# Sliding-window attention and gated MLP layers on one core: masked-Q score tiles, joined bursts and a new order

## Chip, cores and metric

The kernel runs on one NeuronCore of a Trainium2 chip. The metric is device time in microseconds (us) of one execution. The engines are TensorE (PE; its weight loads are listed apart as PEld), VectorE (DVE), ScalarE (ACT), GpSimd (POOL) and SyncE (SP, which here only issues DMAs). Each runs its own instructions in order; between engines they wait on semaphores.

## What is computed

Four layers over x of 2048 tokens by 448 features in bf16: attention (layer 0), MLP (1), attention (2), MLP (3), each on a layer norm of x and added to x. Attention has 16 heads of 28; a token sees itself and 7 earlier tokens at steps of 2.

```python
def attn(x, wqkv, wo):                     # S=2048, D=448, H=16, Dh=28
    q, k, v = split_heads(x @ wqkv)
    idx = pos[:, None] - arange(8) * 2     # 8 keys, every second token
    logits = einsum("hsd,hswd->hsw", q, k[:, idx]) * Dh ** -0.5
    logits = where(idx >= 0, logits, -1e9)
    o = einsum("hsw,hswd->hsd", softmax(logits), v[:, idx])
    return merge_heads(o) @ wo

def mlp(x, w_gate, w_up, w_down):          # F=1792
    return ((x @ w_gate) * (x @ w_up)) @ w_down

x = x + attn(layernorm(x), wqkv, wo)
x = x + mlp(layernorm(x), w_gate, w_up, w_down)
x = x + attn(layernorm(x), wqkv, wo)
x = x + mlp(layernorm(x), w_gate, w_up, w_down)
```

## The kernel before

**Layout and tiles.** Tokens are stored with the even ones first and then the odd ones, so that a step of 2 becomes a step of 1 and the window is the 8 last rows of one half. x lies in SBUF for the whole run. The features (448 = 7 x 64) are contracted in slices of 64, so nearly all matmuls use half of PE's rows: two matmuls, one on rows 0 to 63 and one on rows 64 to 127, run at the same time into two PSUM banks. This is the mode that the code calls `MAIN` ("R64", tiles of 64 rows by 128 columns). `twin` and `twin_blocks` build such pairs and `crossed` chains them, so that after the first half of a pair's slices the two row halves swap outputs. Their instructions are recorded at L698 (Q, K and V projections) and L714 (output projection with `wo_g`, down projection with `WD`). The gate and up matmuls (L983, `b_chunk`) run the same way: 14 units of 7 pairs for each chunk of 256 or 512 tokens.

**Attention.** Queries are handled in 17 blocks of 120 (the first 128), two blocks a group, nine groups a layer. For a group `attn_front` computes the scores: for each of 4 head quadruples, 2 blocks, 2 halves of 64 keys and 4 heads, one matmul (L862) with the 28 rows of one head's K as weights (64 keys as columns) and 64 queries (72 for block 0) moving. That is 64 matmuls in tiles of 28 (32) rows by 64 columns, eight running at once, mode "R32", into four banks (one per head of a quadruple). ACT takes the exponential out of PSUM (L869), DVE multiplies by the band mask `MK` (L879). `attn_back` multiplies by V: 64 matmuls (L896) in tiles of 64 rows by 32 columns, mode "C32". V carries columns of ones, so the sum of the weights comes out beside the values. ACT or DVE copies the result to `O_sb` (L910), DVE adds the overlap (L914), and `norm` spreads the sums (L924, DVE), inverts them by Ln and Exp (L925, L926, ACT) and multiplies (L937, DVE) into `oT`, from which `y_blocks` does the output projection.

**Layer norm and transposes.** `ln_chunk` computes statistics (L630, L632 on DVE; L633, L635 on ACT) and writes the normalized block to a slot of `xn_sb` (L651, DVE). Layers 1 to 3 are transposed by DMA (L654, issued on SP). Layer 0's 16 blocks are transposed by PE, four 128x128 matmuls against `ident` for each (L660, mode "F", one bank), and ACT or DVE copies them to `xnTa` (L666).

**Order.** `SEQ` lists the chunks of layers; `Sched` is a planner that runs while the program is built. Every step is an operation with the engines that may do it, its estimated time, what it depends on, and a priority (by chunk `JP`, by kind `PR`). The planner simulates the engines, and at each moment gives a free engine the ready operation with the lowest priority number; a change of PE's mode costs `SWITCH`. PSUM banks (8) are handed out by the planner (`pick_banks`), SBUF slots by rings (`ring`). The order that comes out is fixed: `emit` writes each engine's instructions in this order, with the waits in front of each operation. PE's instructions of one operation are never mixed with another's.

```python
est = op.est[e]
if e == "pe":
    if mode is not None and op.mode != mode:
        est += self.SWITCH
    mode = op.mode
    n = 2 * len(op.ins)
    credit = min(self.CREDIT, credit + (now - clast) / self.FETCH)
    if n > 40:
        est = max(est, (n - credit) * self.FETCH + (self.HICCUP if n > credit + 40 else 0.0))
```

The head of the program loads x and the weights, and runs 48 warm-up matmuls of 256 columns on zeros (L565).

Of the kernel before, what the change touches and what calls it, by code (L numbers as in the profile page):

```python
# [27 lines left out]
MAIN = "R64"  # L28
PE_T = ("00", "01", "02", "03", "04")
HEAD_LN = 5  # L30
HEAD_P = (-53.71, -30.23, -20.33, -12.94, -19.33)
HOLD_A = 1000.0
HOLD_BA = 2000.0
HOLD_BB = 500.0
HOLD_N = 2
S_EST = 270.0
# [8 lines left out]
NXN_ = 6  # L45
NO = 4
NE_ = 2
NR_ = 3
# [3 lines left out]
PR = {'AV': 8.84, 'rstd': -5.66, 'bn': 0.73, 'N': -2.82, 'Gps': -1.08, 'Tps': 16.85, 'H': 18.16, 'S': 10.61, 'VT': 19.61, 'Ex': 16.77, 'G': -2.93, 'xn': -6.19, 'QK': -6.56, 'Ddps': -26.52, 'V': 22.93, 'x': -0.84, 'lnv': -15.5, 'Oc': -6.51, 'Oa': -6.47, 'R': -19.3, 'VVps': 1.22, 'Yps': -25.3, 'PW': 58.69, 'T': -9.57, 'mv': 2.02, 'Rs': -2.57, 'Rl': 21.52, 'QKps': 4.71, 'E': -7.15, 'wqk': -9.31, 'wqp': -11.53}  # L52
JP = {'A20': -3.02, 'B32': 16.28, 'B34': 16.21, 'A22': 20.13, 'B13': 2.73, 'A21': 6.27, 'B12': -2.81, 'A02': -0.21, 'A03': 4.03, 'B30': 4.3, 'B31': 8.23, 'B10': 21.86, 'B11': -14.15, 'A23': 29.86, 'A04': -0.79, 'B33': 153.62, 'A01': -5.33, 'B14': 4.53, 'A00': -24.6}
# [10 lines left out]
WARM = 18  # L64
FILL = 30
SEED = 190
JITTER = 0
ATT_P = 1.96
A_CAP = 4
# [43 lines left out]
class Op:  # L113
    __slots__ = ("engs", "ins", "est", "deps", "mode", "prio", "acquire", "release", "idx", "eng",
                 "dma", "lat", "after", "start", "end", "seen", "selfd", "tmin")
# [14 lines left out]
class Sched:  # L130
# [6 lines left out]
    SWITCH = 92.0  # L137
    FETCH = 4.17
    CREDIT = 36.0
    HICCUP = 210.0  # L140

    def __init__(self):
        self.ops = []
        self.ready = {}
        self.rng = random.Random(SEED)

    def add(self, engs, ins, est, deps=(), prio=0.0, mode=None, acquire=None, release=(), dma=None, lat=0.0, after=None, selfd=(), tmin=None):
        if isinstance(engs, str):
            engs = (engs,)
        if not isinstance(est, dict):  # L150
            est = {e: float(est) for e in engs}
        op = Op(engs=engs, ins=ins, est=est, deps=[d for d in deps if d is not None], mode=mode, prio=prio,
                acquire=acquire, release=release, idx=len(self.ops), dma=dma, lat=lat, after=after, selfd=set(selfd), tmin=tmin)
# [63 lines left out]

    def schedule(self):
        self.holder = [None] * NBK
# [5 lines left out]
        credit, clast = self.CREDIT, 0.0  # L225
# [6 lines left out]
        for op in self.ops:  # L232
# [9 lines left out]
            if not srcs:  # L242
                for e in op.engs:
                    pend[e].append(op)
        left = len(self.ops)
        now = 0.0
        while left:
            moved = False
            b_ready = any(o.acquire is not None and o.acquire.kind == 1 for o in pend["pe"])
            for e in self.ENGS:  # L250
# [4 lines left out]
                for op in pend[e]:  # L255
                    r = self.ready_at(op, e)
                    if r <= now + 1e-6:
                        cands.append((op.prio, op.idx, op))
# [40 lines left out]
                if best is None:  # L299
                    continue  # L300
                op = best
                op.eng = e
                for x in op.engs:
                    pend[x].remove(op)
                if op.acquire is not None:
                    op.acquire.b = self.pick_banks(op.acquire, now)
                    for b in op.acquire.b:
                        self.holder[b] = op.acquire
                        if self.last_rel[b] is not None:
                            op.deps.append(self.last_rel[b])  # L310
                if op.tmin is not None and e == "sp":
                    gate = [o for o in order["pe"] if o.end + self.PE_LAT <= now and isinstance(o.ins[-1][1], tuple) and o.ins[-1][1] in self.ready]
                    op.deps.append(gate[-1].ins[-1][1])
                est = op.est[e]
                if e == "pe":
                    if mode is not None and op.mode != mode:
                        est += self.SWITCH
                    mode = op.mode
                    n = 2 * len(op.ins)
                    credit = min(self.CREDIT, credit + (now - clast) / self.FETCH)  # L320
                    if n > 40:
                        est = max(est, (n - credit) * self.FETCH + (self.HICCUP if n > credit + 40 else 0.0))
                    credit = max(0.0, credit + est / self.FETCH - n)
                    clast = now + est
                op.start, op.end = now, now + est
                free[e] = op.end
                order[e].append(op)
                for bk, i in op.release:
                    b = bk.b[i]
                    assert self.holder[b] is bk  # L330
                    self.holder[b] = None
                    self.free_at[b] = op.end + self.TAIL[op.eng]
                    key = ("rel", op.idx, b)
                    self.ready[key] = (op, len(op.ins) - 1)
                    self.last_rel[b] = key
                left -= 1
                moved = True
                for u in users.get(op.idx, ()):
                    ndep[u.idx] -= 1
                    if ndep[u.idx] == 0:  # L340
                        for x in u.engs:
                            pend[x].append(u)
# [80 lines left out]
def pe_cols(n):  # L423
    return n / 2.4 + 2.6
# [14 lines left out]
def build(nc, A_x, A_wqkv, A_wo, B_w_gate, B_w_up, B_w_down, out):  # L439
# [52 lines left out]
    def one(fn, key=None):  # L492
        return [(fn, key)]
# [641 lines left out]
```

## Time and profile before

| | before |
|---|---|
| runs | 394.56 us median of 3 (391.71, 394.56, 394.9) |
| profiled execution, span from first to last instruction | 391.9 us |
| DVE busy: 0-10, 10-60, 60-110, 110-250, 250-392 us | 6.3, 46.4, 42.4, 92.2, 83.9 us |
| ACT busy: the same stretches | 4.5, 42.1, 31.4, 67.0, 62.4 us |
| gate and up matmuls (L983) | 1960, 180.5 us |
| down projection (L714, `WD`) | 840, 84.0 us |
| Q and K projection (L698, `WQK`) | 504, 53.5 us |
| output projection (L714, `wo_g`) | 256, 29.1 us |
| V projection (L698, `WV`) | 252, 22.2 us |
| scores (L862) and values (L896) | 1088 each, about 12 us each |
| transposes on PE (L660) | 64, 5.0 us |
| granted TensorE clock | 1.00 in all stretches |

The profile is of one execution. A group's busy time is the union of its instructions' times. Matmuls overlap each other, so the length shown for a matmul is much longer than the time until the next one starts; costs on PE are better read from one start to the next. "Idle before" is the time that an engine stood before an instruction, with what ended it; "issue" stands for time in which it waited for nothing that the profile shows. "PE's weight loads" are separate instructions, one before each matmul.

### The profile page before, as it was taken

The page shows a single profiled execution, that of the slowest core. Times are in us where ns is not written, and L with a number is a line of the kernel's source. Part 1 is how long each engine was busy: PE and PEld are TensorE (multiplying, and loading weights), DVE is VectorE, ACT ScalarE, POOL GpSimd, SP SyncE. Part 2 cuts the span into 40 slices and gives each one's busy share as a digit, 9 for nine tenths or more (in the row PEclk, how much of TensorE's full clock was granted, in tenths as well). Part 3 has the DMA queues.
Part 4 walks back from the last instruction along what each step waited for, and adds up shares of the span by engine and source line. Part 5 has one row for each costly group of instructions (what it writes and reads, how often), then busy time and mean ns, then how long its engine had stood idle before and what let it go on. Part 6 is the DMA issues. An engine that isn't in the chain of part 4 may idle for free.

```text
span 391.9 us, 13910 instructions
## 1 busy us (share of the span) xinstructions
PE 384.9 (98%) x6142; PEld 213.8 (55%) x6142; DVE 271.2 (69%) x596; ACT 207.3 (53%) x398; POOL 7.6 (2%) x36
## 2 busy tenths in 40 slices
PE   8999999999999999999999999999999999999997
PEld 6655657545444544554546867444454544444674
DVE  6989899669967765684788645258942689477252
ACT  4888876478523745467651523268315782263230
POOL 6010000000000000000000000000000000000000
DMA  8990161501220401320121141010050102403101
GB/s 275 295 306 19 24 93 28 106 13 30 48 49 15 80 15 35 64 28 15 17 49 21 36 95 29 25 20 11 12 128 7 26 7 47 95 4 16 34 27 47
DMA packets 54703, 22.47 MB, mean 57 GB/s; under 512 B 44836, under 2 KB 54644, under 8 KB 54644
## 3 DMA queue, kind: packets, MB, share of 16 engines
q1 hardware_dynamic: 53284, 19.47, 23.7%
q10 hardware_dynamic: 1360, 2.12, 1.8%
q8 instruction: 48, 0.79, 0.8%
q14 instruction: 11, 0.09, 0.1%
HBM read 8.54 MB, written 2.71 MB: 29 GB/s over the span
## 4 chain that ended last, share of the span: by engine, by line
PE 90%; DVE 4%; DMA 2%; ACT 2%; issue 1%; SPq 0%; DVEq 0%
PE ps L983 41%; PE ps L714 25%; PE ps L698 16%; PE ps L896 3%; PE ps L862 3%; PE ps L1004 1%; DMA xnTb<-xn_sb 1%; DMA x_sb<-in_A_x_dram 1%; PE ps L660 1%; DVE xn_sb L651 1%; DVE st L630 1%; DVE x_sb L954 1%; ACT R_sb L925 1%; ACT R_sb L926 1%; DVE E_sb L879 0%
## 5 line engine op out<-in xcount | busy, mean ns | idle before, releaser
L983 PE MATMUL ps<-xnTb,WGU 64*128 64x512 bf16 (+1 forms) x1960 | 180.5, 333 | 0.9 <-DMA xnTb<-xn_sb 0.9
L983 PEld LDWEIGHTS ps<-xnTb,WGU 64*128 64x128 bf16 x1960 | 93.5, 94 | 73.8 <-ACT g_sb L989 1.5
L989 ACT ACTIVATE g_sb<-ps 128x512 bf16<-128x512 f32 (+1 forms) x140 | 71.4, 511 | 95.0 <-PE ps L983 94.3
L992 DVE TENSOR_TENSOR hT<-g_sb,ps 128x512 bf16<-128x512 bf16 (+1 forms) x140 | 79.3, 574 | 55.1 <-ACT g_sb L989 46.1
L714 PE MATMUL ps<-WD,hT 64*128 64x448 bf16 x840 | 84.0, 349 | 0.1
L714 PEld LDWEIGHTS ps<-WD,hT 64*128 64x128 bf16 x840 | 40.2, 94 | 37.0 <-DVE hT L992 0.8
L698 PE MATMUL ps<-xnTa,WQK 64*128 64x512 bf16 (+1 forms) x504 | 53.5, 353 | 0.3
L954 DVE TENSOR_TENSOR x_sb<-x_sb,ps 128x448 bf16<-128x448 bf16 x62 | 36.2, 614 | 24.9 <-PE ps L714 24.8
L630 DVE BATCH_NORM_STATS2 st<-x_sb 128x6 f32<-128x448 bf16 x64 | 37.5, 615 | 2.7 <-DMA x_sb<-in_A_x_dram 2.7
L869 ACT ACTIVATE E_sb<-ps 128x1024 bf16<-128x1024 f32 (+1 forms) x36 | 33.5, 980 | 9.6 <-PE ps L862 9.3
L750 ACT ACTIVATE qk<-ps 128x1024 bf16<-128x1024 f32 (+1 forms) x30 | 27.1, 921 | 19.3 <-PE ps L698 19.0
L651 DVE TENSOR_SCALAR xn_sb<-x_sb,mv,rstd 128x512 bf16<-128x512 bf16 (+1 forms) x64 | 33.7, 569 | 4.7 <-ACT rstd L635 4.5
L698 PEld LDWEIGHTS ps<-xnTa,WQK 64*128 64x128 bf16 x504 | 23.5, 94 | 24.0 <-ACT xnTa L666 0.8
L879 DVE TENSOR_TENSOR E_sb<-E_sb,MK 128x1024 bf16<-128x1024 bf16 (+2 forms) x40 | 23.9, 613 | 8.8 <-ACT E_sb L869 8.5
L714 PE MATMUL ps<-wo_g,oT 64*128 64x448 bf16 x256 | 29.1, 349 | 0.0
L633 ACT ACTIVATE lnv<-mv,eps_sb 128x2 f32<-128x2 f32 (+1 forms) x33 | 9.5, 293 | 30.4 <-DVE mv L632 30.2
L937 DVE TENSOR_TENSOR oT<-O_sb,R_sb 128x480 bf16<-128x480 f32 (+3 forms) x36 | 22.1, 627 | 3.4 <-ACT R_sb L926 3.1
L925 ACT ACTIVATE R_sb<-R_sb 128x480 f32<-128x480 f32 (+1 forms) x34 | 20.1, 600 | 5.6 <-DVE R_sb L924 5.6
L924 DVE STREAM_SHUFFLE R_sb<-O_sb 128x480 f32<-128x480 f32 (+1 forms) x34 | 22.7, 696 | 0.0
L698 PE MATMUL ps<-WV,xnTa 64*128 64x336 bf16 (+3 forms) x252 | 22.2, 304 | 0.2
L926 ACT ACTIVATE R_sb<-R_sb 128x480 f32<-128x480 f32 (+1 forms) x34 | 20.1, 602 | 0.4
L714 PEld LDWEIGHTS ps<-wo_g,oT 64*128 64x128 bf16 x256 | 12.3, 94 | 11.6 <-DVE oT L937 0.4
(47 smaller groups left out, 170.7 us busy)
## 6 DMA issues: line engine op xcount, KB each, us to landing
out_dram<-x_sb SPq DMA_DIRECT2D x15, 112.0 KB, 1.7
WD<-in_B_w_down_dram SPq DMA_DIRECT2D x2, 784.0 KB, 11.5
WGU<-in_B_w_up_dram SPq DMA_DIRECT2D x2, 784.0 KB, 17.6
WGU<-in_B_w_gate_dram ACTq DMA_DIRECT2D x2, 784.0 KB, 13.3
x_sb<-in_A_x_dram SPq DMA_DIRECT2D x3, 448.0 KB, 6.4
vt<-qk SPq DMA_DIRECT2D x42, 16.0 KB
xnTb<-xn_sb SPq DMA_TRANSPOSE x32, 3.0
x_sb<-in_A_x_dram SPq DMA_DIRECT2D x2, 224.0 KB, 4.2
```

Of the source, the lines that this page charges most:

```text
L630: sc.add("dve", one(lambda E, B=B: E.bn_stats(st6[:, B, :], x_sb[:, B, :]), ("bn", li, B)), 525.0, deps=[("x", li - 1, B)] + ([("xn", li - ...
L651: sc.add("dve", one(lambda E, B=B, dst=dst, src=src: E.tensor_scalar(dst, src, mv[:, B, 0:1], rstd[:, B:B + 1], ALU.subtract, ALU.mult), ( ...
L698: parts[0 if s < 3 else 1][1].append((lambda E, w=w, c=c, lo=lo, st=st, sp_=sp_: E.matmul(u["out"](w), u["lhs"](w, c, lo, lo + 64), u["rhs ...
L714: ins.append((lambda E, w=w, c=c, lo=lo, st=st, sp_=sp_: E.matmul(outs(w), lhs(w, c, lo), rhs(w, c, lo), start=st, stop=sp_), keys[w] if s ...
L750: return E.activation(dst, src, ACT.Copy) if hasattr(E, "activation") else E.tensor_copy(dst, src)
L869: return E.activation(E_sb[:, slot, 2 * hp:2 * hp + 2, 0:w], ps[:, b0:b0 + 2, 0:w], ACT.Exp, scale=SCALE)
L925: sc.add("act", one(lambda E: E.activation(R_sb[:, rs, 0:w], R_sb[:, rs, 0:w], ACT.Ln), ("Rl", li, qb)), act_est(w, False), deps=[("Rs", l ...
L926: sc.add("act", one(lambda E: E.activation(R_sb[:, rs, 0:w], R_sb[:, rs, 0:w], ACT.Exp, scale=-1.0), ("R", li, qb)), act_est(w, False), de ...
L954: sc.add("dve", one(lambda E: E.tensor_tensor(x_sb[:, B, :], x_sb[:, B, :], ps[:, bk[w], 0:D], ALU.add), ("x", li, B)), dve_est(D), deps=[ ...
L983: ins.append((lambda E, u=u, k=k, w=w: E.matmul(u["out"](w), WGU[64 * w:64 * w + 64, k, 128 * u["fc"]:128 * u["fc"] + 128], X[64 * w:64 * ...
L989: sc.add("act", one(lambda E, gs=gs, bk=bk: E.activation(g_sb[:, gs, 0:nt], ps[:, bk[0], 0:nt], ACT.Copy), ("G", li, j, fc)), act_est(nt), ...
L992: sc.add("dve", one(lambda E, gs=gs, bk=bk, fc=fc: E.tensor_tensor(hT[:, fc, hs, 0:nt], g_sb[:, gs, 0:nt], ps[:, bk[1], 0:nt], ALU.mult), ...
```

## The change

- **Scores.** A new DVE operation per group writes `Qz`, two copies of the group's Q, each with the rows of two of the four heads set to zero (`qmask`, a column of ones and zeros per copy; two `tensor_scalar` instructions of 4 x 240 elements). There is one buffer (`NZ` = 1). A score matmul then takes 64 rows of K (two heads) and 32 keys as weights and moves both masked copies, 2 x 64 queries, so that both heads' scores come out side by side. There are still 64 matmuls per group, now in tiles of 64 rows by 32 columns, the same as the values have; `e_at` says where a head's scores lie. Each pair of banks now holds one query block, and the mask product is one instruction per pair for all groups.
- **Bursts.** Scores and values share the mode `BURST`. When the planner picks one of them, it joins up to `JOIN` = 3 that are ready and, if a projection or gate/up operation (the host) is ready too, puts up to `MAXALT` = 3 of its first steps among them. Such a step, a pair of 64x128 matmuls, is issued as 8 matmuls of 64x32 (`pair`, `alt_of`), one to each column strip. All waits of the joined operations stand in front of the first instruction.
- **Planner.** `run_pe` estimates PE's time from a queue of 64 instructions, a time per instruction, a refill time, and blocks of 256 instructions that arrive after `LINE_T`. In place of the rule with `CREDIT`.
- **Transposes of layer 0.** In chunks 1 to 4 (14 of 16 blocks) each 128x128 transpose becomes two of 64 rows, into two banks, in the mode `MAIN`.
- **Slots.** `xn_sb` 6 to 5, `R_sb` 3 to 2. The values' matmuls now wait for their `O_sb` slot (before, the copy did). Dependences on the last of several matmuls become dependences on all of them; gate/up units keep their order (`after`).
- **Order.** New `PR`, `JP`, `HEAD_P`, `HOLD_*`, `ATT_P` (1.96 to 3.0), `A_CAP` (4 to 5), and a new table `XP` that adds its own priority to most single operations. Warm-up: 25 matmuls of 512 columns in place of 48 of 256.

```diff
 MAIN = "R64"
+BURST = "C32"
+JOIN = 3
+MAXALT = 3
+T64 = (1, 2, 3, 4)
-S_EST = 270.0
+S_EST = 448.0
+AV_EST = 288.0
-NXN_ = 6
+NXN_ = 5
-NR_ = 3
+NR_ = 2
+NZ = 1
-WARM = 18
-FILL = 30
+WARM = 9
+FILL = 16
...
+    QUEUE = 64
+    REFILL = 256.0
+    LINE = 256
+    LINE_T = 3900.0
...
+                    if op.mode == BURST:
...
+                        for o in okay:
+                            if o is not op and o.mode == BURST and len(got) < JOIN and fits(o):
+                                take(o)
+                                got.append(o)
+                        short = [(o, n) for o in got for n in range(len(o.ins))]
+                        n, stream = 2 * len(short), sum(o.est[e] for o in got)
+                        host = next((m for m in okay if m not in got and m.mode == MAIN and len(m.alt) and fits(m)), None)
+                        k = 0
+                        if host is not None:
+                            per = host.est[e] / (len(host.ins) / 2)
+                            while k < len(host.alt) and stream + k * per < self.REFILL + (n + 16 * k - self.QUEUE) * self.FETCH:
+                                k += 1
+                        end = self.run_pe(t, n + 16 * k, stream + (k * per if k else 0.0))
...
+def pair(calls):
...
+    def strip(out, lhs, rhs, start, stop, row, c):
+        return lambda E: E.matmul(out()[c:c + 32], lhs()[:, c:c + 32], rhs(), start=start, stop=stop, tile_position=(row, c))
+    ins = [(whole(*a[:5]), a[6]) for a in calls]
+    strips = [strip(*a[:6], c) for a in calls for c in range(0, 128, 32)] if all(a[6] is None for a in calls) else None
+    return ins, strips
...
+                for c in () if wide else range(4):
+                    for h in range(2):
+                        ins.append((lambda E, c=c, h=h, slot=slot, bk=bk: E.transpose(ps[:, bk[h], :].bitcast(bf)[:, 64 * c:64 * c + 64], xn_sb[64 * h:64 * h + 64, slot, 128 * c:128 * (c + 1)],
+                                                                                      ident[64 * h:64 * h + 64, 64 * h:64 * h + 64]), ("Tps", li, B) if (c, h) == (3, 1) else None))
...
+        def fz(E, a):
+            return E.tensor_scalar(Qz[:, zs, a, :, 0:end - tok], qk[:, 1, :, tok:end], qmask[:, a:a + 1], None, ALU.mult)
...
-        for hc, d, c, b in [(hc, d, c, b) for hc in range(4) for d in range(nd) for c in range(2) for b in range(4)]:
+        for hc, d, c, s_, p in [(hc, d, c, s_, p) for hc in range(4) for d in range(nd) for c in range(2) for s_ in range(2) for p in range(2)]:
             ck, nk, cq, nq = qb_info(qbs[d])
...
+            ins.append((lambda E, hc=hc, c=c, s_=s_, p=p, b=b, h=h, ks=ks, qs=qs: E.matmul(
+                ps[64 * c + 32 * s_:64 * c + 32 * s_ + 32, bk[b], 2 * nc * h:2 * nc * (h + 1)], qk[64 * p:64 * p + 64, 0, hc, ks:ks + 32],
+                Qz[64 * p:64 * p + 64, zs, :, hc, qs:qs + nc], start=True, stop=True, tile_position=(64 * p, 64 * c + 32 * s_)), None))
...
-        sc.add("pe", ins, S_EST * nd / 2, deps=deps + [prev], mode="R32", acquire=bk, prio=prio)
+        sc.add("pe", ins, S_EST * nd / 2 * nc / 64, deps=deps + [prev, ("Qz", li, g)], mode=BURST, acquire=bk, prio=prio)
...
-        xslot_users[hs] = [("Gps", li, j, FC - 1), ("Ups", li, j, FC - 1)]
+        xslot_users[hs] = [(k, li, j, fc) for k in ("Gps", "Ups") for fc in range(FC)]
```

## The prediction

> **What bounds the kernel now.** I read the page's busy table, the chain of waits and the instruction queue first. Columns: engine, busy us, share of the span, instructions.
>
> ```profile
> span 391.9 us, 13910 instructions
> PE 384.9 (98%) x6142; PEld 213.8 (55%) x6142; DVE 271.2 (69%) x596; ACT 207.3 (53%) x398; POOL 7.6 (2%) x36
> ...
> q8 instruction: 48, 0.79, 0.8%
> ...
> PE 90%; DVE 4%; DMA 2%; ACT 2%; issue 1%; SPq 0%; DVEq 0%
> ```
>
> TensorE (PE) carries the chain. It issues 6142 matmuls and as many weight loads, 12284 in all; the instruction queue moved 48 packets of 0.79 MB / 48 = 16 KB, so one packet goes with 12284 / 48 = 256 PE instructions: a block.
>
> Next, PE's timeline around attention. Columns: start, length, engine and line, names, tile shape, count, in brackets the idle time.
>
> ```profile
> 86.78 0.54 PE L896 MATMUL ps<-E_sb,v_sb 64*32 64x64 bf16 x47
> 88.09 0.26 PE L896 MATMUL ps<-E_sb,v_sb 64*32 64x64 bf16 x17 [0.78 <-issue]
> 88.28 1.69 PE L983 MATMUL ps<-xnTb,WGU 64*128 64x512 bf16 x14
> ...
> 179.83 3.19 PE L983 MATMUL ps<-xnTb,WGU 64*128 64x512 bf16 x28
> 182.94 0.71 PE L862 MATMUL ps<-qk 28*64 28x64 bf16 x64
> 183.58 4.71 PE L983 MATMUL ps<-xnTb,WGU 64*128 64x512 bf16 x42
> 188.22 0.71 PE L862 MATMUL ps<-qk 28*64 28x64 bf16 x64
> 188.86 3.20 PE L983 MATMUL ps<-xnTb,WGU 64*128 64x512 bf16 x28
> 191.98 1.36 PE L896 MATMUL ps<-E_sb,v_sb 64*32 64x64 bf16 x128
> 193.27 6.22 PE L983 MATMUL ps<-xnTb,WGU 64*128 64x512 bf16 x56
> ```
>
> The wide matmuls cannot get faster: 183.58 to 188.22 holds 21 pairs, 4.64 us less one drain of 0.1, which is 0.216 us a pair and so 0.42 ns a column. The attention bursts can. From 179.83, 14 pairs end at 182.85, the scores start at 182.94 and the next wide matmul at 183.58: one score burst costs 0.09 + 0.64 = 0.73 us. The double value burst costs 0.10 + 1.29, so 0.70 each. At 88.09 a value burst stood 0.78 us for "issue", with no semaphore behind it.
>
> Where a burst's time goes, by counting its matmuls in windows that grow (window, length, PE busy and count, clock, DMA):
>
> ```profile
> 182.90:183.10 0.20, 0.16 (x32) 1.00 0.18 21
> 182.90:183.20 0.30, 0.26 (x35) 1.00 0.22 24
> 182.90:183.30 0.40, 0.36 (x47) 1.00 0.21 23
> 182.90:183.40 0.50, 0.46 (x59) 1.00 0.22 25
> ```
>
> 32 matmuls (64 instructions) start within 0.16 us, then almost none for 0.1 us, then 12 per 0.1 us: 8.3 ns for a matmul and its load. The second half is paced by instruction supply, not by the array.
>
> Last, the other engines by stage, and the DVE groups nearest to the new operation (busy us, mean ns, idle before).
>
> ```profile
> 10.00:60.00 50.00, 48.89 (x1092) 28.94 (x1086) 46.42 (x119) 42.07 (x82) 1.64 (x6) 1.00 0.60 145
> 110.00:250.00 140.00, 140.00 (x2104) 78.21 (x2102) 92.20 (x202) 66.95 (x131) 0.00 (x0) 1.00 0.21 39
> ...
> L651 DVE TENSOR_SCALAR xn_sb<-x_sb,mv,rstd 128x896 bf16<-128x896 bf16 x32 | 22.1, 732 | 2.4 <-ACT rstd L635 2.4
> L651 DVE TENSOR_SCALAR xn_sb<-x_sb,mv,rstd 128x512 bf16<-128x512 bf16 x32 | 11.7, 406 | 2.3 <-ACT rstd L635 2.1
> L573 DVE COPY WQK<-hT 128x448 bf16<-128x448 bf16 x4 | 0.9, 278 | 0.0
> ```
>
> After the PE and weight-load columns come DVE and ACT. Layer 0's attention has DVE at 46.4 and ACT at 42.1 of 50 us; later DVE is at 66%. So the front has little room, the rest much.
>
> **The change, part by part.** All against this profile's 391.9 us.
>
> 1. *Bursts.* 1088 matmuls each of scores and values are 17 bursts of 64. Now 17 x 0.73 + 17 x 0.70 = 24.3, plus what five value bursts took beyond the usual 0.60 (or 1.29 double) from first start to next wide matmul: at 86.78 (1.50) 0.90, at 266.72 (1.65) 0.36, at 312.77 (1.45) 0.16, at 31.45 (0.74) 0.14, at 51.73 (1.39) 0.10: 1.7. Together 26.0. Afterwards a score matmul streams 128 columns instead of 64: 64 x 128 / 8 tiles = 1024 columns x 0.42 = 0.43 us. Values stay; their first 32 show 0.155, so 0.31 for 64. Both now use 64x32 tiles, so a joined pair drains once on the way in (0.10) and once out (0.13): 0.97 us, if the strips of the host projection, 0.216 us of wanted work each, cover the instruction supply. 17 x 0.97 = 16.5, a saving of 9.5. Against it I set block losses: the four double value bursts (256 instructions, as the joined pair) lost 0.10, 0, 0.36 and 0.16, mean 0.155; 17 of them 2.6. Net -6.9. Best end: no losses, -9.5; worst end: the slower rival below.
> 2. *Strips.* Each step replaces 2 matmuls and 2 loads by 8 and 8. Three steps per pair are 51 steps and 51 x 12 = 612 more instructions, 2.4 blocks. No row shows eight concurrent 512-column strips. Nearest: the double value burst, 16 rounds of eight 32-column loads and eight matmuls on these very tiles in 1.29 us, 0.081 a round, of which 0.027 is stream. So a step loses at most 0.054, 2.8 in all; below nothing it cannot go, since a strip streams the same columns. I take 0, since that round was paced by supply.
> 3. *Transposes.* 56 of 64 change. In the timeline 16 take 13.24 to 14.24: 0.0625 each, 3.5 in all, and three entries from wide matmuls drain about 0.1 each. Afterwards 56 pairs of 64 columns, 0.030 each, in the wide mode: 1.7. So -2.1. Their copies read the same 512 columns; two PSUM banks are held instead of one, which I price at 0 up to +1.
> 4. *Masked Q.* 36 added DVE operations (32 of 960 elements, four of 512). Rows: the two-operation tensor_scalar goes from 406 to 732 ns over 384 elements, so 785 at 960; single-source copies, 278 at 448 and 169 at 64, give about 400. The new one has one operation, as the copy: 400, at most 14.4 us in all; upper end 28.3. Mask products fall from 40 to 36 (eight of 420 become four of 690): -0.6. PE waits for them only if DVE is late. In 10 to 60 us lie five groups: 4.0 against 3.6 free. ACT has 7.9 free and may take copies out of PSUM. I charge +1; from 0 to 7.9 - 3.6 = +4.3. Without that cover the whole 4.0 is paid.
> 5. *Added waits.* One Q buffer: a mask product on DVE waits for the previous group's scores, and x updates and layer norms queue behind it. A joined burst takes all its waits first, the host's and the value's O slot included; behind them stands all of PE. Fewer xn (5) and R (2) slots hold DVE earlier.
> 6. *New order*, which also moves every DMA on SP's queue (x loads, 48 DMA transposes, 49 strips of K and Q, 27 of V, outputs). PE's waits outside bursts: 0.9 at 75.75 for a DMA transpose, 0.6 before a score burst, 0.5 in the head, and the loads' waits of 0.4 or less, about 1. I take half of these 3 us away: -1.5; from -3 to +4, since as much can be put in.
>
> Warm-up columns stay (48 x 256 against 25 x 512). Sum: 391.9 - 6.9 - 2.1 + 1 - 1.5 = 382.4. That profile lies at the low end of the three runs (391.71 to 394.9, median 394.56), and the same spread upward is kept in the range.
>
> [...] For the Q product the rows above give 400 ns. [...] For the strips the round of 0.081 us bounds the weight loads. [...]
>
> **Rivals.**
> - *The strips rarely attach* (no projection ready just then, so the change doesn't do what it says). A joined pair is then 256 unaided instructions, as the double value burst: 1.39 against 1.43 now. Only parts 3, 4 and 6 are left: 391.9 - 0.7 - 2.1 + 1 - 1.5 = 388.6, up to 392. For it: a host must be ready and find banks beside a score's four. Against: wide matmuls surround every burst.
> - *DVE ends the front.* At 785 ns, without relief from ACT and with none of the 3.6 us idle usable (it is scattered in front of results of ACT and PE), layer 0 pays all 7.9 between 10 and 60: 382.4 - 1 + 7.9 = 389.3. For it: DVE's 46.4 of 50. Against: copies can move to ACT.
> - *Blocks run out inside joined bursts*, the slower end. A joined pair with three steps is 256 + 48 = 304 instructions, three bursts more still, so it can cross two block edges within 1.3 us. The longest loss at one edge is 0.90. Two of them in two of three bursts: 11.3 x 1.8 = 20.3, less the 2.6 counted: 400. It decides above (398.5 - 382.4 + 2.6) / 17 = 1.1 us a burst. For it: the losses at 86.78 and 266.72. Against: the double burst at 191.98 lost nothing.
>
> **How the numbers follow.** Forecast 0.62; no strips 0.10; DVE front 0.12; blocks 0.16. Range 374 to 395: down to no block losses (-2.6), all waits gone (-1.5), triple joins and the lower Q price, up to both middle rivals plus the spread of runs; that leaves out the blocks and a tail of 0.04. Under 1% (390.6 to 398.5) a measurement of this kernel can tell little from no change. Faster: 0.62 plus most of the first rival and a third of the second, 0.72; within 1% 0.13; slower 0.15.
>
> **What would show it.** Right: few bursts, each with scores and values in one stretch of 64x32 tiles and 512-column strips among them, about 0.97 us of extra time per pair; narrow transposes of about 0.12 us a block; Q products near 0.4 us; PE still at 98%. Wrong: PE idle for "issue" inside joined bursts (blocks), PE waiting on the Q product or on DVE before 110 us, strip steps longer than 0.22 us, or new PE stands on DMA transposes.

## The result and the profile after

The changed kernel takes 412.93 us (median of 5 runs, 410.21 to 413.31) against 394.56 for the kernel before (391.71 to 394.9): a ratio of 1.048, 95% interval 1.0435 to 1.0517. The forecast was 382 with a range of 374 to 395.

First the page of the changed kernel: span, busy table (engine, busy us, share of the span, instructions), the granted clock in 40 slices of 10.2 us, and the chain that ended last.

```profile
span 408.5 us, 14476 instructions
PE 384.5 (94%) x6415; PEld 214.6 (53%) x6415; DVE 287.0 (70%) x638; ACT 205.6 (50%) x394; POOL 7.5 (2%) x35
PEclk9965999999999999999999999999999999999999
PE 87%; DMA 4%; SPq 4%; ACT 2%; DVE 1%; issue 1%
```

PE is busy for as long as before (384.5 against 384.9 us) in a span that is 16.6 us longer. So the change hardly shortened PE's work, and it put in time in which PE does nothing: the idle times before PE's matmuls sum to 21.4 us, against 4.6 before. DMA and SP's queue have 8% of the chain, against 2%, and the clock falls to 0.6 and 0.5 in two slices of the head. The timeline of PE and DVE shows where (start, length, engine, line, operation, count, idle before with its releaser):

```profile
16.61 2.97 PE L534 MATMUL ps<-xnTa,WQK 64*128 64x512 bf16 x26
...
33.16 0.63 DVE L758 BATCH_NORM_STATS2 st<-x_sb 128x6 f32<-128x448 bf16 x1 [8.77 <-DMA x_sb<-in_A_x_dram]
34.16 0.39 PE L793 MATMUL ps<-ident,xn_sb 64*128 64x64 bf16 x8 [14.58 <-DVE xn_sb L779]
34.37 1.89 PE L534 MATMUL ps<-xnTa,WQK 64*128 64x512 bf16 x8
36.06 0.42 PE L793 MATMUL ps<-ident,xn_sb 64*128 64x64 bf16 x8
```

From 19.6 to 34.16 us PE has nothing to do. The engine named is DVE, but DVE stood as well, for a load of x. The same stretch in SP's queue, from the timeline of its DMA issues:

```profile
8.41 0.62 SPq L626 DMA_DIRECT2D x_sb<-in_A_x_dram  x1
...
15.17 5.70 SPq L626 DMA_DIRECT2D wo_g<-in_A_wo_dram  x1
20.91 0.39 SPq L626 DMA_DIRECT2D x_sb<-in_A_x_dram  x1
21.35 2.46 SPq L626 DMA_DIRECT2D WGU<-in_B_w_up_dram  x1
```

The loads of x blocks 8 to 11 and 12 to 15 are issued at 8.41 and 20.91 and land at 21.42 and 33.14. Before, they were issued at 4.50 and 6.82, ahead of all loads of `wo_g`, `WD` and `WGU`, and landed at 10.94 and 13.21. Now weights stand before them, and one `wo_g` issue held the queue for 5.70 us. The windows around the stand give PE's busy time and count and the same for its weight loads, DVE, ACT and POOL, then the granted clock, DMA share and GB/s:

```profile
20.00:30.00 10.00, 0.00 (x0) 0.00 (x0) 2.95 (x9) 2.39 (x5) 0.00 (x0) 0.63 1.11 251
30.00:40.00 10.00, 5.84 (x72) 2.38 (x74) 4.71 (x15) 2.73 (x5) 0.00 (x0) 0.51 0.49 120
```

DMA ran at 251 GB/s while PE stood, and PE came back at half its clock: the eight matmuls at 34.37 take 1.7 us until the next entry, 0.42 a pair, where 0.216 is usual.

What PE's work consists of, from each matmul's start to the next one's, idle time left out (us; the column e8 is an experiment below, the changed kernel with the loads in the old order):

| | before | after | e8 |
|---|---|---|---|
| wide pairs | 345.5 | 340.0 | 339.7 |
| steps in strips (320 matmuls, 40 steps) | 0 | 7.8 | 7.8 |
| scores | 11.0 | 11.7 | 11.5 |
| values | 11.2 | 8.8 | 9.0 |
| layer 0's transposes | 4.3 | 2.9 | 2.7 |
| warm-up and the last down projections | 12.7 | 13.0 | 12.7 |
| sum | 384.7 | 384.3 | 383.4 |
| idle before matmuls | 4.6 | 21.4 | 8.1 |

The bursts hardly ever joined: a value burst and a score burst stand next to each other once (50.84 and 51.44 us), without strips, and two value bursts once (312.11), with three steps. Both met a stand for "issue", the first four matmuls behind the bursts, the second inside them, in PE's timeline:

```profile
50.84 0.68 PE L1044 MATMUL ps<-E_sb,v_sb 64*32 64x64 bf16 x64 [0.71 <-ACT qk L889]
51.44 0.73 PE L1011 MATMUL ps<-Qz,qk 64*32 64x128 bf16 x64
...
53.96 1.93 PE L534 MATMUL ps<-WV,xnTa 64*128 64x448 bf16 x16 [1.30 <-issue]
...
314.66 0.24 PE L1044 MATMUL ps<-E_sb,v_sb 64*32 64x64 bf16 x12 [0.95 <-issue]
```

All others are single, the scores mostly with no step or one, the values mostly with two.

### The profile page after: what moved, and what is told of

The parts are those of the page before. It is cut to its first block, busy times and chain, and to the rows that moved or that the text cites. A ratio compares the mean times of both kernels' runs of the same rounds, so it can differ in the third digit from the quotient of the medians.

```text
span 408.5 us, 14476 instructions
## 1 busy us (share of the span) xinstructions
PE 384.5 (94%) x6415; PEld 214.6 (53%) x6415; DVE 287.0 (70%) x638; ACT 205.6 (50%) x394; POOL 7.5 (2%) x35
## 4 chain that ended last, share of the span: by engine, by line
PE 87%; DMA 4%; SPq 4%; ACT 2%; DVE 1%; issue 1%
PE ps L534 79%; DMA x_sb<-in_A_x_dram 4%; SPq L626 4%; PE ps L1011 2%; PE ps L1044 2%; PE ps L537 2%; PE ps L1150 1%; ACT qk L889 1%; ACT E_sb L1019 1%; DVE st L758 0%; DVE xn_sb L779 0%; DVE R_sb L1069 0%; DVE v_sb L981 0%; ACT R_sb L1071 0%; PE ps L793 0%
## 5 line engine op out<-in xcount | busy, mean ns | idle before, releaser
L534 PE MATMUL ps<-xnTb,WGU 64*128 64x512 bf16 (+1 forms) x1920 | 175.6, 333 | 0.1
L534 PEld LDWEIGHTS ps<-xnTb,WGU 64*128 64x128 bf16 x1920 | 92.3, 94 | 70.3 <-issue 1.1
L1135 ACT ACTIVATE g_sb<-ps 128x512 bf16<-128x512 f32 (+1 forms) x140 | 70.5, 512 | 103.3 <-PE ps L534 78.1
L534 PE MATMUL ps<-WD,hT 64*128 64x448 bf16 x818 | 82.9, 349 | 0.0
L534 PE MATMUL ps<-xnTa,WQK 64*128 64x512 bf16 (+1 forms) x496 | 54.7, 363 | 1.1 <-POOL WQK L701 0.5
L779 DVE TENSOR_SCALAR xn_sb<-x_sb,mv,rstd 128x896 bf16<-128x896 bf16 (+1 forms) x64 | 33.8, 568 | 2.8 <-ACT rstd L763 2.7
L889 ACT ACTIVATE qk<-ps 128x1024 bf16<-128x1024 f32 (+1 forms) x27 | 24.7, 930 | 13.4 <-PE ps L534 13.1
L1026 DVE TENSOR_TENSOR E_sb<-E_sb,MK 128x1024 bf16<-128x1024 bf16 (+1 forms) x36 | 23.2, 658 | 5.5 <-ACT E_sb L1019 5.3
L534 PE MATMUL ps<-WV,xnTa 64*128 64x336 bf16 (+3 forms) x246 | 23.2, 304 | 1.4 <-issue 1.3
L1055 ACT ACTIVATE O_sb<-ps 128x512 f32<-128x512 f32 (+2 forms) x22 | 11.7, 558 | 15.8 <-PE ps L1044 15.8
## 6 DMA issues: line engine op xcount, KB each, us to landing
x_sb<-in_A_x_dram SPq DMA_DIRECT2D x3, 448.0 KB, 12.2
```

The lines of the kernel that those rows point to most:

```text
L534: return lambda E: E.matmul(out(), lhs(), rhs(), start=start, stop=stop)
L779: sc.add("dve", one(lambda E, B=B, dst=dst, src=src: E.tensor_scalar(dst, src, mv[:, B, 0:1], rstd[:, B:B + 1], ALU.subtract, ALU.mult), ( ...
L889: return E.activation(dst, src, ACT.Copy) if hasattr(E, "activation") else E.tensor_copy(dst, src)
L1026: return E.tensor_tensor(e, e, MK[:, kind, 0:nc].unsqueeze(1).unsqueeze(1).to_broadcast([128, 2, w // nc, nc]), ALU.mult)
L1135: sc.add("act", one(lambda E, gs=gs, bk=bk: E.activation(g_sb[:, gs, 0:nt], ps[:, bk[0], 0:nt], ACT.Copy), ("G", li, j, fc)), act_est(nt), ...
```

## The experiments

In all of them the order of the instructions on each engine is that of the kernel they start from, except for what is named; only lines behind the planner's last step, or the named instruction itself, were edited. Beside the first four the kernel before took 392.99 us, beside the others 393.71; the ratios are to these.

**e1: the two loads of x ahead of the weights.**

```diff
     sc.schedule()
+    late = [e for e in sc.order["sp"] if tag(e)[:2] == ("x", -1) and tag(e)[2] >= 8]
+    rest = [e for e in sc.order["sp"] if e not in late]
+    at = next(i for i, e in enumerate(rest) if tag(e)[0] == "wo")
+    sc.order["sp"] = rest[:at] + late + rest[at:]
```

> The changed kernel with one edit: the two loads of x blocks 8 to 15 stand on SP's queue in front of the output and MLP weights; every other engine keeps its order. Theory A (these two loads, behind weights, make the loss): the 14.6 us stand of PE before 34.2 us goes, and with it the half clock after it (12 pairs at 0.43 instead of 0.216 us, 2.6 us). 408.5 - 14.6 - 2.6 gives a span near 391, a time of 391 to 394, about the kernel before. Theory B (the front is held by DVE or by instruction supply, and the loads only show it): another wait takes the place and the time stays above 402. Theory C (the forecast's bursts and transposes hold, only the loads spoil them): 383 or less.

Measured: 399.39 us, ratio to before 1.0157 (1.013 to 1.0184). Moving two DMA issues gave back 13.5 us of the 18.4 (12.0 when each time is taken against the kernel before run beside it). The time lies between theories A (391 to 394) and B (above 402), so the two loads are most of the loss and not all. PE's idle time falls from 21.4 to 10.7 us, and its time without idle is the same within 0.2. What is left has another name, in PE's timeline:

```profile
21.51 1.04 PE L534 MATMUL ps<-xnTa,WQK 64*128 64x512 bf16 x8 [0.45 <-issue]
...
29.86 0.80 PE L534 MATMUL ps<-xnTa,WQK 64*128 64x512 bf16 x5 [1.14 <-issue]
...
38.35 0.64 PE L1044 MATMUL ps<-E_sb,v_sb 64*32 64x64 bf16 x60 [2.85 <-issue]
...
41.93 2.29 PE L534 MATMUL ps<-WV,xnTa 64*128 64x448 bf16 x10 [1.32 <-issue]
```

PE stands 5.8 us in these four for "issue", with no semaphore behind it; three of the four are in plain projections, not in bursts, but the last of these comes four matmuls behind the value and the score burst that stand next to each other.

**e2: the kernel before, with the loads in the order of after.**

```diff
     sc.schedule()
...
+    sc.order["sp"] = rest[:n] + wo[:2] + by["d_wd0"] + by["d_wu0"] + by["d_x2"] + by["d_wd1"] + wo[2:3] + by["d_one"] + wo[3:] + by["d_x3"] + by["d_wu1"] + rest[n:]
```

> The kernel before with one edit: the same two x loads and the weights stand on SP's queue in the changed kernel's sequence. Theory A: PE stands for the late x here too, 10 to 17 us, so 402 to 409. Theory B: the order before tolerates it, under 397.

Measured: 404.58 us, ratio 1.0293 (1.0244 to 1.0342), 11.6 us more than before. PE waits 9.4 us for `xn_sb`, against 0.5; its longest, from PE's timeline:

```profile
21.34 1.89 PE L660 MATMUL ps<-ident,xn_sb 128*128 128x128 bf16 x16 [7.87 <-DVE xn_sb L651]
```

So the late loads are shown from both sides: taken out of after they give 13.5 us back, put into before they cost 11.6, with nothing else of the change present.

**e3: e1 without strips.** The host's steps are issued as wide pairs behind the burst.

```diff
+    for i, (got, seq) in enumerate(sc.order["pe"]):
+        if any(not isinstance(n, int) for _, n in seq):
+            host = got[-1]
+            short = [(o, n) for o, n in seq if o is not host]
+            sc.order["pe"][i] = (got, short + [(host, n) for n in range(len(host.ins))])
```

> As the first, but the host's steps inside bursts are issued as pairs behind the burst, in the same order. By the trace of the changed kernel a value burst costs 0.70 us alone and about 0.60 with two strip steps, a score burst 0.76 alone and 0.73 with one: 1 to 2 us slower than the first run if that is all. The forecast's reading (the strips hide the whole instruction supply, 0.4 us a burst pair): 5 us slower or more. Strips worth nothing: within 0.5 us.

Measured: 398.38 us, 1.0123 (1.0088 to 1.0157), not told apart from e1, where 1 to 2 us slower was expected. From the first gate/up matmul to the end, a stretch behind most of the head's stands, it needs 333.46 us against 332.68: by this, one profile of each, the strips are worth about 0.8 us.

**e4: e1 without the Q products.** The scores are taken from Q itself.

```diff
-                Qz[64 * p:64 * p + 64, zs, :, hc, qs:qs + nc], start=True, ...
+                qk[64 * p:64 * p + 64, 1, hc, qs + tok:qs + tok + nc].unsqueeze(1).to_broadcast([64, 2, nc]), start=True, ...
...
+    sc.order["dve"] = [e for e in sc.order["dve"] if tag(e)[0] != "Qz"]
```

> As the first, without the masked copies of Q: scores are taken from Q itself, so two heads' scores are added up and the 36 DVE operations (14.7 us) are left out. Theory A: DVE is not what ends the path, within 1.5 us of the first run. Theory B (DVE ends the front): 4 us faster or more.

Measured: 398.19 us, 1.0123 (1.0089 to 1.0157). The 36 Q products, 14.7 us of DVE, cost within 1.2 us of nothing; from the first gate/up matmul on, 0.1 us more without them than with (332.76 against 332.68).

**e8: the first 20 DMAs of SP's queue in the order of before.** In e1 the two loads came early, but the last weights landed at 38.24 us; with the old order they land sooner (31.3 in the profile of before).

```diff
     sc.schedule()
+    want = [("x", -1, 0), ("x", -1, 2), ("stg", 1), ("stg", 3), ("x", -1, 4), ("wv", 0), ("wv", 1), ("x", -1, 8), ("stv", 0), ("stv", 1), ("x", -1, 12),
+            ("wo", 0), ("wo", 1), ("wo", 2), ("wo", 3), ("wd", 0), ("wd", 1), ("wu", 0), ("wu", 1), ("vones",)]
+    head = [next(e for e in sp if tag(e) == t) for t in want]
+    sc.order["sp"] = head + [e for e in sp if e not in head]
```

> The changed kernel with SP's first 20 DMAs in the order of the kernel before (all of x, then the output weights, then the MLP weights); all else as changed. With only the two x loads moved, 399.4 was left, and PE stood 6.3 us for 'issue' with no semaphore, five sixths of it at 28 to 42 us, with half clock after it; the last MLP weights landed at 38.2 instead of 31.3 us. Theory D (PE's own instruction blocks come late while weights stream): weights end near 31, about half of the stands go, 394 to 397. Theory E (the stands come from how many instructions the new bursts need at once, whatever the DMA does): 399 as before.

Measured: 395.66 us (10 runs), 1.0059 (1.0026 to 1.0092). The order of the loads as a whole is worth 17.3 us of the 18.4 (16.4 against the kernel before run beside each). The other parts of the change together leave the kernel 0.3 to 0.9% slower than before.

**e9: e1 with less weight traffic early.** Both `WD` loads and the second `WGU` up load are held until the first stores of V's strips.

```diff
+    held = [e for e in sc.order["sp"] if tag(e) in (("wd", 0), ("wd", 1), ("wu", 1))]
+    rest = [e for e in sc.order["sp"] if e not in held]
+    at = next(i for i, e in enumerate(rest) if tag(e)[0] == "PW") + 1
+    sc.order["sp"] = rest[:at] + [held[i] for i in sorted(range(3), key=lambda i: tag(held[i])[0] != "wu")] + rest[at:]
```

> As the run with the two x loads in front, and three of the four MLP weight loads of SP (both down-projection halves, the second half of up) wait behind the first stores of V strips, about 40 us. Theory D: no weights stream at 28 to 40 us, the stands there go (5 us and the half clock, about 2), 391 to 393, if the weights still arrive before the first gate/up matmul near 58. Theory E: 399. If the weights come too late: over 400 with PE waiting for a DMA near 58.

Measured: 397.39 us, 1.0106 (1.0062 to 1.0151). The stands at 38.35 and 41.93 (4.2 us together) shrink to one of 1.86, and a new one of 3.96 us comes at 47.37, in the stretch where the held loads now run (206 GB/s from 40 to 50 us, against 5 in e1). So the long stand follows the loads; that of 1.86 comes at the same matmul as the one at 41.93 in e1, behind the two adjacent bursts, though the loads ran at only 58 GB/s from 30 to 40 us. The time is that of neither theory, 391 to 393 or 399.

**e10: e8 with the scores of before.** Tiles of 28x64, no Q products, no strips in score bursts.

```diff
-            ins.append((lambda ...: E.matmul(ps[64 * c + 32 * s_:64 * c + 32 * s_ + 32, ...], qk[64 * p:64 * p + 64, 0, hc, ks:ks + 32], Qz[64 * p:64 * p + 64, zs, :, hc, qs:qs + nc], ...
+            ins.append((lambda ...: E.matmul(ps[64 * c:64 * c + 64, bk[b], o:o + nc], qk[32 * b:32 * b + DH, 0, hc, ks:ks + 64], qk[32 * b:32 * b + DH, 1, hc, qs:qs + nc], ...
```

> SP's head as before, and scores as before: 28 rows by 64 keys from Q itself, no masked copies, steps of a host behind a score burst instead of in it; values, transposes and order as changed. By the traces a score burst of the new kind costs 0.73 to 0.76 us, of the old kind 0.73: within 1.5 us of the run with SP's head as before. The forecast's 0.97 for a joined pair against 1.43 would make it 5 us slower or more.

Measured: 396.48 us, 1.0077 (1.0052 to 1.0102): the new score tiles are not told apart from the old ones. (It has 60 matmuls fewer, so block edges, treated below, move too: a stand of 1.23 us at 232.66 has come, and e8's of 0.56 at 300.58 has gone.)

**e11: e8 with all transposes 128x128.**

```diff
-                        ins.append((lambda ...: E.transpose(ps[:, bk[h], :].bitcast(bf)[:, 64 * c:64 * c + 64], xn_sb[64 * h:64 * h + 64, slot, ...
+                    ins.append((lambda ...: E.transpose(ps[:, bk[0], :].bitcast(bf)[:, 128 * c:128 * (c + 1)], xn_sb[:, slot, ...
```

> SP's head as before, and all of layer 0's transposes 128x128 again (one bank of the two used), order as changed. The forecast gave the narrow ones 2.1 us: 2 us slower than the run with SP's head as before. If the front is held by instruction blocks instead, fewer instructions (112 fewer) help: 0 to 2 us faster.

Measured: 395.69 us, 1.0062 (1.0034 to 1.0089), as e8. Its PE work is 2.1 us longer (385.6 against 383.4), and its idle time 1.7 us shorter (6.5 against 8.1). That does not show the narrow transposes to be worth nothing: e11 also has 112 instructions fewer in the head. Its stands for "issue" lie elsewhere, e8's of 1.83 us is gone and one of 1.68 has come at 46.60, and the next two runs show what such a shift alone can move.

**e12 and e15: where the "issue" stands come from.** In e8, the first nine (e12) or four (e15) warm-up matmuls of 512 columns are each issued as eight of 64, so that 63 or 28 more matmuls stand ahead of all work.

```diff
+        def wf(E, n=n):
+            if n < WARM:
+                for m in range(7):
+                    E.matmul(ps[:, wb[0], 64 * m:64 * m + 64], warm[:, 0:128], warm[:, 0:64], start=True, stop=True)
+                return E.matmul(ps[:, wb[0], 448:512], warm[:, 0:128], warm[:, 0:64], start=True, stop=True)
+            return E.matmul(ps[:, wb[0], :], warm[:, 0:128], warm, start=True, stop=True)
```

> The kernel with the head of SP's queue in the order of before (e8), and nine 512-column warm-up matmuls each issued as eight of 64 columns: 63 matmuls and 63 weight loads more, 126 PE instructions, before any real work; the rest of PE's order is unchanged. Reading so far: in the kernels with this front, the long stands for 'issue' come at the same matmul numbers, counted from the first on PE (221, 346, 473, 601, 728; 125 to 128 apart, so 250 to 256 instructions), whatever work is there, about 1.3 to 1.7 us after an instruction packet ended. Theory D (PE runs out of instructions at a block edge while the loads fill the DMA engines): the stands stay at these numbers, so they move to work that lies 63 matmuls earlier; those of e8 at 28.89 and 38.22 us vanish from there, none is at number 664, and the time moves by up to 3 us either way from e8's ratio of 1.006 (below 1.000 if the new edges fall between bursts). Rival E (something in that work itself, a wait the profile doesn't show): the long stand stays before the same value projection, now number 664, and the ratio stays within 1.003 to 1.009.

> As the shift of 126 instructions, but four warm-up matmuls only: 28 matmuls and 28 weight loads more, 56 instructions. Theory D: stands at numbers 221, 346, 473, 601, 728, none at 629 (601 + 28); the ratio differs from that of e8 and from that of the larger shift by up to 3 us, since each offset puts other work at the edges. Rival E: the long stand at 629 and a ratio of 1.003 to 1.009.

Measured: e12 398.04 us, 1.0115 (1.0092 to 1.0138); e15 398.62 us, 1.0127 (1.0104 to 1.015). An edit that touches only matmuls on zeros, before anything of the program's own, costs 2.4 to 3 us. The warm-up is longer by 0.4 us at most: the first transpose starts at 9.53 and 9.97, against 9.58 in e8. PE's timeline of e12 has these stands of over 0.5 us for "issue" up to 52 us:

```profile
26.03 0.19 PE L799 MATMUL ps<-ident,xn_sb 64*128 64x64 bf16 x1 [0.55 <-issue]
...
34.94 0.29 PE L1017 MATMUL ps<-Qz,qk 64*32 64x128 bf16 x4 [3.78 <-issue]
...
50.83 0.30 PE L1017 MATMUL ps<-Qz,qk 64*32 64x128 bf16 x14 [1.23 <-issue]
```

Against the trace's records of the instruction queue, worked out for each stand: the running number of the matmul on PE, and the end of the last instruction packet before it.

| kernel | matmul | starts | stand | packet ended |
|---|---|---|---|---|
| before | 347 | 25.48 | none | 24.24 |
| before | 1741 | 88.09 | 0.78 | 86.70 |
| after | 601 | 53.96 | 1.30 | 52.64 |
| e1 | 221 | 21.51 | 0.45 | 19.75 |
| e1 | 346 | 29.86 | 1.14 | 28.37 |
| e1 | 473 | 38.35 | 2.85 | 36.92 |
| e1 | 601 | 41.93 | 1.32 | 40.46 |
| e8 | 601 | 38.22 | 1.83 | 36.87 |
| e9 | 728 | 47.37 | 3.96 | 45.87 |
| e12 | 347 | 26.03 | 0.55 | 24.54 |
| e12 | 474 | 34.94 | 3.78 | 33.39 |
| e12 | 856 | 50.83 | 1.23 | 49.40 |
| e15 | 346 | 30.94 | 3.45 | 29.37 |
| e15 | 601 | 43.02 | 0.42 | 41.67 |

The numbers are the same within one in all kernels with this head, whatever work falls on them, and 125 to 128 apart; the value projection that stood 1.83 us in e8 as matmul 601 does not stand as 664 or 629. So the stands belong to the edges of blocks of 256 instructions (128 matmuls and their loads; the instruction queue of after and e8 moved 50 packets for PE's 12830 instructions, 257 to a packet), and each ends 1.3 to 1.8 us after an instruction packet has landed. PE has run out of instructions. There are two ways to it. The packets come late: while the weights are loading, e1's packets that end at 28.37 and 36.92 start 5.6 and 5.7 us after PE passed the edge before, e9's that ends at 45.87 7.1 us after it, those of before at the first two of these numbers 3.7 and 3.5; later most start 2 us after it or less. And a block can be used up too fast: the block from 473 to 601 holds the two adjacent bursts. In after, e1, e8 and e9 the next packet starts only 0.9 to 1.2 us behind the edge, PE has used the block up 1.8 to 2.3 us behind it, and each time it stands at 601, for 1.30, 1.32, 1.83 and 1.86 us. So the largest stand left in e8 is that of a joined burst, not of a late packet.

Where the block edges fall moves the time by 2.4 to 3 us in these two runs, as much as e8's whole rest of 2.0 us. So this rest is no measure of what the other parts of the change are worth.

**e13: the prices of bursts by themselves.** Behind e8's last matmul a row of test patterns, eight times each, with 14 wide pairs of 512 columns after each.

```diff
+        for _ in range(8):
+            for b, k in ((S0(), 0), (S(), 0), (V(), 0), (S(), 1), (V(), 2), (V() + S(), 0), (V() + S(), 3)):
+                ins += mix(b, k) + M(14)
```

> The kernel e8 with a test row behind its last matmul, on data that is there and without reading the results: eight times the seven patterns old scores (28x64 tiles), new scores (64x32, 128 columns), values, scores with one projection step in strips, values with two, values and scores joined, values and scores joined with three steps, each followed by 14 wide pairs of 512 columns. The program's time is longer by the test row, some 220 us. Price of a pattern: its period less 14 wide pairs, and less 0.216 us for each step in strips. My forecast's prices: old scores 0.73, values 0.70, joined with three steps 0.97 and 0.155 of block losses. Theory F (the forecast's price was right, joins only did not come about): joined with three steps 0.95 to 1.15, so 0.3 to 0.5 saved a pair. Rival G (instructions cost their supply whatever lies beside them, and a join saves one change of tile shape only): joined without steps 1.25 to 1.4, with three 1.15 to 1.35. New scores alone 0.73 to 0.80, with one step 0.70 to 0.78; values with two steps 0.58 to 0.65.

Measured: from a pattern's first start to the next one's, less 14 x 0.216 = 3.02, less 0.216 for each step. Two patterns in PE's timeline, values and scores joined without steps and with three:

```profile
409.23 0.68 PE L1254 MATMUL ps<-E_sb,v_sb 64*32 64x64 bf16 x64
409.72 0.75 PE L1244 MATMUL ps<-Qz,qk 64*32 64x128 bf16 x64
410.40 3.20 PE L1259 MATMUL ps<-xnTb,WGU 64*128 64x512 bf16 x28
413.52 0.31 PE L1254 MATMUL ps<-E_sb,v_sb 64*32 64x64 bf16 x32
...
416.39 0.28 PE L1244 MATMUL ps<-Qz,qk 64*32 64x128 bf16 x10 [1.06 <-issue]
416.61 3.20 PE L1259 MATMUL ps<-xnTb,WGU 64*128 64x512 bf16 x28
419.73 0.71 PE L1249 MATMUL ps<-qk 28*64 28x64 bf16 x64
```

The first: 413.52 - 409.23 - 3.02 = 1.27. The second: 419.73 - 413.52 - 3.02 - 0.65 = 2.54, with a stand at a block's edge. All eight of each:

| pattern | price, us | forecast |
|---|---|---|
| old scores | 0.74 | 0.73 |
| new scores | 0.77 | |
| values | 0.71 | 0.70 |
| new scores, one step | 0.76 | |
| values, two steps | 0.61 | |
| joined, no step | 1.27 | |
| joined, three steps | 1.27 in four, 1.55, 1.67, 2.53, 2.54: mean 1.67 | 0.97, and 0.155 for blocks |

The patterns below three steps agreed within 0.02 in all eight. A join saves 0.21 us against the two bursts (1.27 against 0.77 + 0.71), and three steps among them add nothing to that, where the forecast had 0.30 more. How a step is placed seems to matter: in the values with two steps, parts of 21 matmuls take 0.09 and 0.08 us until the next step, in the joined pattern parts of 32 take 0.23 to 0.26, about 8 ns a matmul, close to the 8.3 ns read from the second half of a score burst in before. Why the steps covered the short parts and not the long ones was not tested. With its block losses the joined burst costs more than old scores and values apart, 1.67 against 1.45; in the test row it follows another joined burst by 3 us, so the losses are those of this row.

## Why the prediction was wrong

The step that failed is part 6, the new order, in its words "which also moves every DMA on SP's queue (x loads, ...)" with the bounds "from -3 to +4". The size and the sign were both wrong: e1 shows +13.5 us for two loads of x behind weights, e8 17.3 for all of the loads' order. The prediction named the x loads and did not follow them. The diff had what was needed: the table `XP` puts +6.57 and +29.7 on operations 11 and 12, which are these two loads, and the planner gives each load a constant latency (`XL`, 5.0 and 5.5 us for these two), however many are in the queue; they took 13.0 and 12.2 from issue to landing. So the planner saw little of what this order costs. The upper bound of +4 was taken from the sizes of waits in the old profile, where these loads were early; a bound from the loads would have been the time until the weights ahead of them had landed.

1. *Bursts, -6.9*: the term was wrong twice. The joined price of 0.97 is 1.27 when no block edge falls into it and 1.67 in the mean; had all 17 pairs joined at that price, the term would have been 28.4 - 26.0 = +2.4. The error is in the words "if the strips of the host projection cover the instruction supply": among parts of 32 matmuls they covered none of it (1.27 with three steps as without), among parts of 21 0.10 us for two steps. And but for two the joins did not come about. What came instead, single bursts with 40 steps, is in the table of PE's work: scores +0.5 to +0.7, values -2.2 to -2.4, and 7.8 us of strips for about 7.5 us of wide pairs (17840 columns at 0.42 ns), so about -1.4.
2. *Strips, 0*: right as a price (scores with one step 0.76 against 0.77, values with two 0.61 against 0.71).
3. *Transposes, -2.1*: on PE 1.4 to 1.6, two thirds to three quarters of it; whether it reaches the end is open, since e11 moves the block edges too.
4. *Masked Q, +1*: at most about that. An operation of 960 elements took 464 ns, between the 400 taken and the upper row of 785, and one of 512 took 344; an estimate from these two sizes is 0.27 ns an element and 207 ns fixed. No run shows the "lower Q price" that the low end of the range counts on; what the runs showed are these 464 and 344 ns. e4 shows no cost on the path.

```profile
L1000 DVE TENSOR_SCALAR Qz<-qk,qmask 128x960 bf16<-128x960 bf16 x32 | 13.5, 464 | 2.5 <-PE ps L1011 2.0
```

5. *Added waits*: they ended no stand of note. The Q product waits 2.0 us in all for the scores that free its one buffer, and nothing on PE waits for it.

Of the rivals, "the strips rarely attach" had the right fact under the wrong name (joins are rare, strips are not), and "DVE ends the front" did not happen. "Blocks run out inside joined bursts" had its mechanism right: both joined bursts that came about met a stand at a block's edge, of 1.30 and 0.95 us in after and of 1.83 and 0.56 in e8, where it had taken 0.90 as the longest. Its cost is small because there were two joins and not 17, and it did not have the head, where packets came late while loads ran (up to 7.1 us after PE had passed the edge before, e9). Of the signs of being wrong, "PE idle for "issue" inside joined bursts" came at 314.66, and "PE waiting ... on DVE before 110 us" at 34.16, there for a load behind DVE.

e8's rest against before, 394.4 - 391.9 = 2.5 us of span, is in the head. There PE's idle time is 7.4 us up to 60 us, against 2.7; later it is 0.8 against 1.9. Of the 7.4, 2.1 stand for "issue" (before: none), 1.82 stand before a transpose at 9.58 that waits for DVE's `xn_sb` (before: 0.49), and 0.71 before the adjacent bursts for `qk` from ACT. Between 20 and 60 us the wide pairs take 3.8 us beyond their columns, against 1.9, at a granted clock of 0.63 from 38 to 42 us, after the stand of 1.83. In the rest of the program the change gains: PE's work is 1.3 us shorter in all, with this loss of 1.9 in it. No variant run here beats the kernel before. Joins forced into the real order were not tried, so whether an order with many joins exists stays open; by e13 one could gain 0.21 us where no block edge falls into it.

## What to carry to other kernels

Before pricing anything on the busiest engine, list the first DMA issues of the new order beside the old one and ask what each load now stands behind; a planner that gives a load a fixed latency can move it behind weights and report no cost (here 5.0 and 5.5 us planned, 13.0 and 12.2 taken). A burst of short instructions was paid here by its instructions (about 8 ns a matmul in the parts of 32 in e13): price it by the instructions it holds and where the block edges fall, and count what is mixed into it as cover only as far as a run shows it. Work saved on an engine can be worth nothing in a stretch where that engine waits for loads or instructions (PE's work in e8 is 1.3 us shorter than before, its idle time 3.5 us longer), so ask stage by stage what ends last there.

## What the runs showed of the hardware

- PE's instructions came in blocks of about 256 (48 packets for 12284 in before, 50 for 12830 in after), the stands at their edges were 125 to 128 matmuls apart, and where PE stood for a block, it went on 1.3 to 1.8 us after the packet had landed (1.32 in after, 1.76 in e1). While loads ran at 152 to 224 GB/s in windows of 10 us, packets started up to 5.7 (e1) and 7.1 us (e9) after PE had passed the edge before, and PE stood up to 3.96 us (e9). A block that PE used up in 1.8 to 2.3 us ended in a stand even with the next packet started 0.9 to 1.2 us behind its edge (the adjacent bursts in after, e1, e8 and e9). An edit of nothing but the number of warm-up instructions moved the time by 0.6 to 0.7% (e12 and e15 against e8).
- The granted clock fell with stands of PE: 0.63 and 0.51 in the windows from 20 to 30 and 30 to 40 us, around the one of 14.58 us in after, where the pairs behind it took 0.42 us each, and 0.63 in e8's window from 38 to 42 us, after one of 1.83 us.
- Eight weight loads of 32 columns and eight 512-column matmuls in 64x32 tiles, put among a burst's matmuls, cost no more than the two wide matmuls that they replace: with 0.216 us taken off for each step, scores with one step took 0.76 us against 0.77 without, values with two 0.61 against 0.71, and the joined pattern with three 1.27 against 1.27 (e13, where no stand at a block's edge fell into it).
